# Three blocks of 512 tokens in place of four of 384 at the end of an attention-and-MLP kernel

## The chip, the cores and the metric

The kernel runs on one core of a Trainium2 chip. The metric is device time in microseconds (us), the median of several runs of the compiled program. Engines are named as in the profile: PE is TensorE (PEld its weight loads), DVE VectorE, ACT ScalarE, POOL GpSimd, SP SyncE, which issues nearly all DMAs here. Instructions of one engine start in the order in which they stand.

## What is computed

```python
# attention: 4 sequences of 768 tokens, 8 heads of 64; chunks of 32 queries, each with its own keys:
# 8 memory keys, 16 tokens to the left, the chunk itself, 8 tokens to the right (cut off at the ends)
scores = scale * np.matmul(q_c, k_full.transpose(0, 1, 3, 2))
a = np.exp(scores - np.max(scores, axis=-1, keepdims=True))
a = a / (np.sum(a, axis=-1, keepdims=True) + 1e-09)
out[:, :, c_start:c_end] = np.matmul(a, v_full)
# x: 3072 tokens x 512, then the MLP with 2048 hidden columns
h = x @ w_in
g = (a[0] + a[1]*h + a[2]*h**2 + a[3]*h**3) / (1 + abs(b[0])*abs(h) + abs(b[1])*h**2 + 1e-6)
return (g @ w_out).astype(np.float32)
```

All is float32 in and out. Weights and activations are split into a high and a low part, and each product of the MLP is three matmuls (high by high, low by high, high by low).

## The kernel before

**Blocks and steps.** The 3072 tokens are 8 blocks of 384, numbered 0 to 7. The hidden columns are 16 tiles of 128. One *step* n takes one block through one tile of hidden columns; there are 128 steps. Blocks 0 and 1 are done in two halves (10 and 6 tiles), so the order is: 0 and 1 (first ten tiles), 2, the rest of 1 (steps 36 to 41), the rest of 0 (42 to 47), then block 3 (48 to 63), 4 (64 to 79), 5, 6 and 7 (112 to 127).

**What one step does.** `g1(n)` is the in-projection: 12 matmuls (4 slices of 128 rows of x, 3 products each) that write the bank `h`, 128 hidden columns by the tokens of the block. The *chain* of step n makes g from h: ACT `chain_abs` (|h| and a line of it), POOL `chain_below` (the denominator, `cy`), ACT `chain_line` and DVE `chain_above` (the numerator, two instructions that read h), ACT `chain_inverse` (Ln and Exp, the reciprocal `cr`), DVE `chain_ratio` (three instructions that read the reciprocal), POOL `chain_hi` and `chain_lo` (`ghi`, `glo`, the split of g). `g2(n)` is the out-projection: for each 128 tokens three matmuls of 512 output columns into an accumulator `o`, with ghi, ghi and glo in that order. When a block's 16 tiles are through, `evac` copies the accumulators to a stage buffer and DMAs it out.

**The order, from step 30 on**, is written out in one loop, and all instructions are pinned to it:

```python
for n in range(HAND, LAST):
    g2(n - 2)
    attend(n, "db")          # attention on PE: values of one pair of heads, scores of another
    attend(n, "qv")          # loads
    g1(n + 1)
    ...
    chain_abs(n); chain_below(n); chain_line(n)     # evac of tiles `early` stands behind these
    chain_above(n); chain_inverse(n)                # evac of the other tiles behind these
    chain_ratio(n)
    chain_hi(n - 1); chain_lo(n - 1)
    attend(n, "xhlencmQ")
```

So PE runs g2(n-2), then g1(n+1), while the other engines work at the chain of n. The last six steps stand in `FINAL`, in the same manner.

**Attention between the steps.** From block 3 on the attention of a block is made while earlier blocks are in the MLP, one *unit* for each of its four pairs of heads. Its pieces, by the letters that `attend` takes: b scores (PE), m maximum and two subtractions (DVE), x exponential (ACT), c transpose on DVE and four DMAs that put the blocks in place, d values (PE), n normalisation (DVE: two small instructions for the reciprocal of the sum, two products), e transpose and DMAs, h and l the split of x (ACT, POOL). `BASES`, `LEAD`, `WHEN`, `AFTER` and `SOON` give each piece its step. A *visit* is a step in which PE has values or scores between g2 and g1; from step 40 on there are 18, of which the last two (101 and 105) have values alone. The values carry a column of ones, whose product is the sum over keys. Q, q and v load a unit's queries and keys into one half of the tile `qk_pairs` (by turns) and its values into one of four half tiles `v_main`.

**Banks.** Eight banks of 512 floats per partition: three for `o`, two for `h` (by turns), one for `cr`, two for `pairs` (scores and values).

Of the kernel before, what the change touches and what calls it, by code (L numbers as in the profile page):

```python
# [12 lines left out]
F32 = mybir.dt.float32  # L13
# [6 lines left out]
CHUNK = 32  # L20
# [12 lines left out]
BLOCKWISE = 3  # L33
BASES = {3: [30, 32, 35, 37], 4: [40, 42, 46, 50]}
# [25 lines left out]
LAST = 122  # L60
# [10 lines left out]

@with_exitstack
def attn_moe(ctx, tc, qk, vm, w, ab, out):
    nc = tc.nc
    P = 128
    NBLK, NPAIR = qk.shape[:2]
    NJT, DM = w.shape[0], out.shape[1]
    D = DM // (2 * NPAIR)
    TB = out.shape[0] // NBLK
    NC = TB // CHUNK  # L80
    NG = TB // P
    KEYS = P // 2
    NK, NQ, NV = start_of(NC - 1) + KEYS, NC * CHUNK, NC * (D + 1)
    NCT = DM // P
# [6 lines left out]
    st = ctx.enter_context(tc.tile_pool(name="st", bufs=3))  # L91
# [22 lines left out]
    v_mains = [const.tile([P, 2, NV], F32, name=f"v_main{i}") for i in range(2)]  # L114
# [187 lines left out]
    def pair_max(i, p):  # L302
        u = unit[i, p]
        sv = u.pop("s")
        mx = sm.tile([P, 2, NG], F32, name="mx")
        pin(nc.vector.tensor_reduce(mx, sv, axis=AX.X, op=ALU.max))
        e = u["e"] = at.tile([P, NG, KEYS, 2], F32, name="e", tag="e", bufs=2)
        turned = e.rearrange("x g w h -> x g (w h)").rearrange("x g (b h k) -> x g b h k", b=4, h=2)
        for h in range(2):
            pin(nc.vector.tensor_tensor(turned[:, :, :, h], sv[:, h].rearrange("x g (b k) -> x g b k", b=4),  # L310
                                        mx[:, h].unsqueeze(2).unsqueeze(3).broadcast_to([P, NG, 4, KEYS // 4]), op=ALU.subtract))

    def pair_values(i, p):
        u = unit[i, p]
        ov = u["o"] = two_banks("o", D + 1)
# [429 lines left out]
```

## Time and profile before

| | |
|---|---|
| device time, median of 3 runs | 618.96 us (618.54 to 621.61) |
| span of the profiled execution, first to last instruction | 617.3 us |
| busy share of the span | PE 98%, PEld 86%, DVE 79%, ACT 71%, POOL 70% |

The profile shows one execution; its own device time isn't listed beside its span, and the median of the runs lies 1.7 us above that span. An engine's busy time is the union of its instructions. Where the mean time of a matmul is shown, it is from start to end, and matmuls overlap: the time that PE needs for each is read from the starts.

### The profile page before, as it was taken

The numbers are of one execution on the slowest core, as the hardware profiler recorded it, in microseconds if no ns is written. First come the engines' busy times: TensorE is split into PE (matmuls) and PEld (weight loads), VectorE is DVE, ScalarE is ACT, GpSimd is POOL, SyncE is SP. The second block draws the span as 40 slices with busy tenths as digits, with TensorE's granted clock in tenths as the row PEclk, the third lists the DMA queues.
The fourth block names the chain that finished last, engine by engine and source line by source line (L and its number), as shares of the span: only waits on it lengthen the run. The fifth ranks groups of instructions, "written<-read, shape, count | busy, mean of one in ns | idle before, by whom it ended". The sixth has DMA issues, their size and how long they took to land.

```text
span 617.3 us, 14116 instructions
## 1 busy us (share of the span) xinstructions
PE 602.5 (98%) x5275; PEld 531.3 (86%) x5275; DVE 490.2 (79%) x959; ACT 435.6 (71%) x822; POOL 433.2 (70%) x459
## 2 busy tenths in 40 slices
PE   7699999999999999999999999999999999999997
PEld 5478789899888888889889898888989888989996
DVE  6799998898867889788778787777878777666674
ACT  5699888798756766666667766676676766676674
POOL 2569987879966667666767766766767676776773
PEclk9999999999999999999999999999999999999999
DMA  8979437103023564342221422242112310010001
GB/s 261 362 267 357 171 104 258 51 1 145 2 83 86 180 209 146 119 132 81 82 81 35 122 68 72 81 133 82 47 54 69 98 27 14 14 52 2 0 1 51
DMA packets 42787, 64.81 MB, mean 105 GB/s; under 512 B 25696, under 2 KB 25696, under 8 KB 42336
## 3 DMA queue, kind: packets, MB, share of 16 engines
q1 hardware_dynamic: 41856, 60.61, 30.7%
q10 hardware_dynamic: 576, 1.74, 0.9%
q0 software_dynamic: 288, 1.57, 0.8%
q8 instruction: 41, 0.67, 0.5%
q14 instruction: 26, 0.21, 0.1%
HBM read 46.60 MB, written 9.44 MB: 91 GB/s over the span
## 4 chain that ended last, share of the span: by engine, by line
PE 28%; issue 28%; POOL 27%; DVE 6%; DMA 5%; ACT 3%; SPq 1%; POOLq 0%; DVEq 0%
PE o L468 13%; PE h L453 13%; POOL glo L542 11%; POOL ghi L535 10%; POOL cy L509 3%; DMA w_raw<-in_w_dram 2%; POOL x_lo L431 2%; DMA out_dram<-stage 2%; POOL w_hl L189 1%; SPq L124 1%; DMA v_main<-in_vm_dram 1%; DVE ct L528 1%; PE pa L393 1%; DVE ct L518 1%; DVE ct L530 1%
## 5 line engine op out<-in xcount | busy, mean ns | idle before, releaser
L453 PE MATMUL h<-x_hi,w_hl 128*128 128x384 f32 x1024 | 265.4, 340 | 1.0 <-DVE ct L519 0.5
L468 PE MATMUL o<-w_hl,ghi 128*128 128x512 f32 x768 | 239.6, 393 | 0.0
L509 POOL TENSOR_TENSOR cy<-cy,ha 128x384 f32<-128x384 f32 x128 | 130.6, 1020 | 140.1 <-ACT cy L505 135.4
L453 PEld LDWEIGHTS h<-x_hi,w_hl 128*128 128x128 f32 x1024 | 185.6, 188 | 12.5 <-DVE ct L519 2.1
L453 PE MATMUL h<-x_lo,w_hl 128*128 128x384 f32 x512 | 172.6, 337 | 0.0
L468 PEld LDWEIGHTS o<-w_hl,ghi 128*128 128x128 f32 x768 | 141.8, 188 | 20.9 <-POOL glo L542 0.4
L468 PE MATMUL o<-w_hl,glo 128*128 128x512 f32 x384 | 151.3, 394 | 0.1
L542 POOL TENSOR_TENSOR glo<-ct,ghi 128x384 fp32r<-128x384 f32 x127 | 129.1, 1017 | 8.9
L504 ACT ACTIVATE ha<-h 128x384 f32<-128x384 f32 x128 | 62.9, 492 | 91.7 <-PE h L453 87.2
L518 DVE TENSOR_TENSOR ct<-ct,h 128x384 f32<-128x384 f32 x128 | 70.5, 551 | 58.4 <-ACT ct L514 58.2
L528 DVE SCALAR_TENSOR_TENSOR ct<-ct,par,cr 128x384 f32<-128x384 f32 x128 | 78.5, 613 | 38.5 <-ACT cr L524 37.5
L535 POOL TENSOR_TENSOR ghi<-ct,zero 128x384 fp32r<-128x384 f32 x127 | 105.6, 831 | 3.7 <-DVE ct L530 2.6
L523 ACT ACTIVATE cr<-cy 128x384 f32<-128x384 f32 x128 | 63.2, 494 | 58.9 <-POOL cy L509 54.5
L453 PEld LDWEIGHTS h<-x_lo,w_hl 128*128 128x128 f32 x512 | 96.2, 188 | 0.0
L505 ACT ACTIVATE cy<-ha,bab 128x384 f32<-128x384 f32 x128 | 91.0, 711 | 4.2
L468 PEld LDWEIGHTS o<-w_hl,glo 128*128 128x128 f32 x384 | 72.0, 187 | 21.1 <-POOL glo L542 1.9
L514 ACT ACTIVATE ct<-h,par 128x384 f32<-128x384 f32 x128 | 84.2, 658 | 0.1
L519 DVE SCALAR_TENSOR_TENSOR ct<-ct,par,h 128x384 f32<-128x384 f32 x128 | 78.7, 615 | 4.5
L530 DVE SCALAR_TENSOR_TENSOR ct<-cr,ct 128x384 f32<-128x384 f32 x128 | 71.4, 558 | 4.4
L529 DVE SCALAR_TENSOR_TENSOR cr<-cy,cr 128x384 f32<-128x384 f32 x128 | 71.0, 555 | 0.0
L524 ACT ACTIVATE cr<-cr 128x384 f32<-128x384 f32 x128 | 60.8, 475 | 4.0
L189 POOL TENSOR_TENSOR w_hl<-w_raw,w_hl 128x512 fp32r<-128x512 f32 x32 | 42.2, 1321 | 7.3 <-ACT w_hl L184 7.3
(65 smaller groups left out, 409.2 us busy)
## 6 DMA issues: line engine op xcount, KB each, us to landing
w_raw<-in_w_dram SPq DMA_DIRECT2D x26, 512.0 KB, 6.9
v_main<-in_vm_dram SPq DMA_DIRECT2D x20, 390.0 KB, 4.7
qk_pairs<-in_qk_dram SPq DMA_DIRECT2D x16, 424.0 KB, 4.0
out_dram<-stage SPq DMA_DIRECT2D x24, 256.0 KB, 3.2
qk<-in_qk_dram SPq DMA_DIRECT2D x24, 212.0 KB, 5.2
v_main<-in_vm_dram SPq DMA_DIRECT2D x20, 195.0 KB, 5.8
eT<-blocks SPq DMA_DIRECT2D x80, 48.0 KB, 2.0
xf<-blocks SPq DMA_DIRECT2D x80, 48.0 KB, 2.0
```

What stands on the lines that cost most here:

```text
L453: pin(nc.tensor.matmul(h[:, :TB], lhsT=wt[:, cols], rhs=xt[i][:, ct, :], start=m == 0, stop=m == last))
L468: ins = nc.tensor.matmul(o, lhsT=gt[:, cols], rhs=wt, start=begin and m == 0, stop=end and m == 2)
L505: pin(nc.scalar.activation(c["y"], c["ha"], AF.Identity, scale=B1, bias=B0))
L509: pin(nc.gpsimd.tensor_tensor(c["y"], c["y"], c.pop("ha"), op=ALU.mult))
L514: pin(nc.scalar.activation(c["t"], c["h"], AF.Identity, scale=A3, bias=A2))
L518: pin(nc.vector.tensor_tensor(t, t, h, op=ALU.mult))
L519: pin(nc.vector.scalar_tensor_tensor(t, t, A1, h, op0=ALU.add, op1=ALU.mult))
L528: pin(nc.vector.scalar_tensor_tensor(t, t, A0, r, op0=ALU.add, op1=ALU.mult))
L529: pin(nc.vector.scalar_tensor_tensor(r, yy, QC, r, op0=ALU.add, op1=ALU.mult))
L530: pin(nc.vector.scalar_tensor_tensor(t, r, 2.0, t, op0=ALU.subtract, op1=ALU.mult, reverse0=True))
L535: pin(nc.gpsimd.tensor_tensor(ghi, chain[z]["t"], zero.broadcast_to([P, TB]), op=ALU.add))
L542: pin(engine.tensor_tensor(glo, chain.pop(z)["t"], gh[z].bitcast(F32), op=ALU.subtract))
```

## The change

The last 1536 tokens become three blocks of 512 (`WIDE = 4`: blocks 4, 5 and 6); blocks 0 to 3 stay at 384. There are 112 steps; blocks 4, 5 and 6 have steps 64 to 79, 80 to 95 and 96 to 111. In a wide step the bank `h` is filled, and g2 has four accumulators; the fourth takes the bank that was `cr`. The reciprocal of a wide step is written over `h` itself, and from step 98 (`FREE`) into the `pairs` bank, which has no attention left. A wide unit has 16 chunks. With its values no column of ones is loaded, because the normalisation's reciprocal comes from a sum over the exponentials on DVE (`pair_sums`, letter z); keys that don't exist at the ends of a sequence are set to zero on POOL (`absent`). In wide steps some attention pieces stand at other places of the loop, and the pieces of three units of block 4 are given steps by hand (`ALONE`). To make room, the stage buffers are one tile and the free ends of `v_main` and `qk_pairs`; `v_main` are two rooms and not four; a wide unit's queries and keys take the whole of `qk_pairs`; the DMA scratch is 1 KB; and x of block 0, which is kept in DRAM for a while, is loaded back by ACT's queue and not POOL's (`x_move`).

```diff
+WIDE = 4
+BLOCKS = [384] * WIDE + [512] * 3
-WHEN = dict(b=0, m=1, x=2, c=2)
+WHEN = dict(b=0, m=1, x=2, c=2, z=3)
-SOON = {3: (dict(m=0, x=1, c=1), dict(e=1, h=4, l=4)), 4: (dict(m=0), {})}
+SOON = {3: (dict(m=0, x=1, c=1), dict(e=1, h=4, l=4)), 4: (dict(m=0, z=3), {})}
+ALONE = {(4, 0): dict(z=45), (4, 1): dict(m=44, x=45, c=45, z=47, h=56, l=56), (4, 2): dict(x=49, c=51, z=52)}
-LAST = 122
+LAST = 106
+FREE = 98
...
-                pin(nc.gpsimd.dma_start(out=t, in_=d))
+                pin(nc.scalar.dma_start(out=t.bitcast(F32), in_=d.bitcast(F32)))
...
+    def pair_sums(i, p):
+        if i < WIDE:
+            return
...
+        for h in range(2):
+            pin(nc.vector.tensor_reduce(sums[:, h], turned[:, h], axis=AX.XY, op=ALU.add))
+        u["rinv"] = inverse_of(sums.unsqueeze(3), n)
...
     def chain_inverse(y):
-        r = chain[y]["r"] = ps_r.tile([P, 512], F32, name="cr", tag="cr")[:, :TB]
+        i = order[y][0]
+        r = chain[y]["h"]
+        if i < WIDE:
+            r = ps_r.tile([P, 512], F32, name="cr", tag="cr")[:, :TB]
+        elif y >= FREE:
+            r = ps_pairs[0].tile([P, 2, 512], F32, name="pairs", tag="pairs")[:, 0]
+        chain[y]["r"] = r
         pin(nc.scalar.activation(r, chain[y]["y"], AF.Ln, bias=QC))
         pin(nc.scalar.activation(r, r, AF.Exp, scale=-1.0))
...
-        early = {True: [0, 1], False: [0]}[order[n - 2][0] < 2]
+        early = [0] if order[n - 2][0] in (2, 3) else [0, 1]
         chain_abs(n)
         chain_below(n)
         chain_line(n)
+        wide = order[n][0] >= WIDE
+        if wide:
+            attend(n, "xh")
         if done_block:
             evac(*done_block, early)
         chain_above(n)
+        if wide:
+            attend(n, "czm")
         chain_inverse(n)
...
-        attend(n, "xhlencmQ")
+        attend(n, "lenQ" if wide else "xhlenczmQ")
```

On PE, in the last steps, the end of one in-projection and the out-projection behind it were, before (h and o are the banks, x_hi and x_lo the split x, w_hl the split weights; a step has the pair of h rows four times):

```order
L453 MATMUL h<-x_hi_103,w_hl 128x384 x2
L453 MATMUL h<-x_lo_105,w_hl 128x384
L468 MATMUL o_7418<-w_hl,ghi 128x512 x2
L468 MATMUL o_7418<-w_hl,glo 128x512
L468 MATMUL o_7419<-w_hl,ghi 128x512 x2
L468 MATMUL o_7419<-w_hl,glo 128x512
L468 MATMUL o_7420<-w_hl,ghi 128x512 x2
L468 MATMUL o_7420<-w_hl,glo 128x512
```

On PE, at the same place of a wide step, they are now:

```order
L510 MATMUL h<-x_hi_102,w_hl 128x512 x2
L510 MATMUL h<-x_lo_104,w_hl 128x512
L526 MATMUL o_6729<-w_hl,ghi 128x512 x2
L526 MATMUL o_6729<-w_hl,glo 128x512
L526 MATMUL o_6730<-w_hl,ghi 128x512 x2
L526 MATMUL o_6730<-w_hl,glo 128x512
L526 MATMUL o_6731<-w_hl,ghi 128x512 x2
L526 MATMUL o_6731<-w_hl,glo 128x512
L526 MATMUL o_6732<-w_hl,ghi 128x512 x2
L526 MATMUL o_6732<-w_hl,glo 128x512
```

The 12 matmuls into h are 512 columns wide and not 384; the out-projection has four accumulators of three matmuls, and no shape of it changed.

On DVE, the step that holds a unit's maximum was, before (ct is the numerator and then g, cr the reciprocal, e the scores less their maximum, mx):

```order
L518 TENSOR_TENSOR ct<-ct,h 128x384
L519 SCALAR_TENSOR_TENSOR ct<-ct,par,h 128x384
L528 SCALAR_TENSOR_TENSOR ct<-ct,par,cr 128x384
L529 SCALAR_TENSOR_TENSOR cr<-cy,cr 128x384
L530 SCALAR_TENSOR_TENSOR ct<-cr,ct 128x384
L306 TENSOR_REDUCE mx<-pairs 128x6
L310 TENSOR_TENSOR e<-pairs,mx 128x12x16 x2
```

On DVE, the same step of a wide block is now:

```order
L591 TENSOR_TENSOR ct<-ct,h 128x512
L592 SCALAR_TENSOR_TENSOR ct<-ct,par,h 128x512
L333 TENSOR_REDUCE mx<-pairs 128x8
L337 TENSOR_TENSOR e<-pairs,mx 128x16x16 x2
L607 SCALAR_TENSOR_TENSOR ct<-ct,par,h 128x512
L608 SCALAR_TENSOR_TENSOR h<-cy,h 128x512
L609 SCALAR_TENSOR_TENSOR ct<-h,ct 128x512
```

The reciprocal is read from h, and the maximum moved from behind the ratio to between the numerator and the ratio.

On DVE, at the end of step 42 and in step 43, where block 1's accumulators are added to their kept halves (stage), there stood before (xt is the normalised result, blocks what a transpose writes):

```order
L331 TENSOR_TENSOR xt<-pairs,rinv 128x3x16x4 x2
L364 STREAM_TRANSPOSE blocks<-e 128x384
L306 TENSOR_REDUCE mx<-pairs 128x6
L310 TENSOR_TENSOR e<-pairs,mx 128x12x16 x2
L492 SCALAR_TENSOR_TENSOR stage<-o_2862,stage 128x512
L492 SCALAR_TENSOR_TENSOR stage<-o_2863,stage 128x512
L518 TENSOR_TENSOR ct<-ct,h 128x384
```

On DVE, at that place, there stand now:

```order
L374 TENSOR_TENSOR xt<-pairs,rinv 128x3x16x4 x2
L421 STREAM_TRANSPOSE blocks<-e 128x512
L559 SCALAR_TENSOR_TENSOR v_main_100<-o_2860,v_main_100 128x512
L559 SCALAR_TENSOR_TENSOR v_main_101<-o_2861,v_main_101 128x512
L591 TENSOR_TENSOR ct<-ct,h 128x384
```

The maximum of unit (4, 1) and its two subtractions left this place; they stand behind the ratio of step 44 now.

## Rows read from the trace of the kernel before

**Rows 1.** The page, busy time of each engine.
```profile
PE 602.5 (98%) x5275; PEld 531.3 (86%) x5275; DVE 490.2 (79%) x959; ACT 435.6 (71%) x822; POOL 433.2 (70%) x459
```

**Rows 2.** Timeline, PE, 521 to 613 us: start, duration, engine, line, operation.
```profile
521.32 0.51 PE L453 MATMUL h<-x_hi,w_hl 128*128 128x384 f32 x2
...
585.97 0.62 PE L468 MATMUL o<-w_hl,ghi 128*128 128x512 f32 x2
...
588.03 0.51 PE L453 MATMUL h<-x_hi,w_hl 128*128 128x384 f32 x2
...
603.07 0.63 PE L468 MATMUL o<-w_hl,ghi 128*128 128x512 f32 x2
...
613.08 0.39 PE L468 MATMUL o<-w_hl,glo 128*128 128x512 f32 x1
```

**Rows 3.** Timeline, PE, around a full visit and one with values alone.
```profile
406.27 0.62 PE L468 MATMUL o<-w_hl,ghi 128*128 128x512 f32 x2
...
411.75 0.63 PE L468 MATMUL o<-w_hl,ghi 128*128 128x512 f32 x2
...
514.24 0.62 PE L468 MATMUL o<-w_hl,ghi 128*128 128x512 f32 x2
...
516.39 0.73 PE L318 MATMUL pairs<-v_main,eT 64*32 64x65 f32 x48
517.04 0.62 PE L453 MATMUL h<-x_hi,w_hl 128*128 128x384 f32 x2
...
519.24 0.63 PE L468 MATMUL o<-w_hl,ghi 128*128 128x512 f32 x2
```

**Rows 4.** Timeline, ACT, POOL and DVE, one step behind its h; brackets: idle time, releaser.
```profile
586.16 0.49 ACT L504 ACTIVATE ha<-h 128x384 f32<-128x384 f32 x1 [0.80 <-PE h L453]
...
587.30 0.65 ACT L514 ACTIVATE ct<-h,par 128x384 f32<-128x384 f32 x1
...
587.48 1.02 POOL L509 TENSOR_TENSOR cy<-cy,ha 128x384 f32<-128x384 f32 x1 [1.27 <-ACT cy L505]
...
587.99 0.56 DVE L518 TENSOR_TENSOR ct<-ct,h 128x384 f32<-128x384 f32 x1 [0.91 <-ACT ct L514]
...
588.45 0.84 POOL L535 TENSOR_TENSOR ghi<-ct,zero 128x384 fp32r<-128x384 f32 x1
588.53 0.50 ACT L523 ACTIVATE cr<-cy 128x384 f32<-128x384 f32 x1 [0.58 <-POOL cy L509]
588.58 0.61 DVE L519 SCALAR_TENSOR_TENSOR ct<-ct,par,h 128x384 f32<-128x384 f32 x1
...
589.37 1.01 POOL L542 TENSOR_TENSOR glo<-ct,ghi 128x384 fp32r<-128x384 f32 x1
589.57 0.62 DVE L528 SCALAR_TENSOR_TENSOR ct<-ct,par,cr 128x384 f32<-128x384 f32 x1 [0.37 <-ACT cr L524]
...
590.69 0.56 DVE L530 SCALAR_TENSOR_TENSOR ct<-cr,ct 128x384 f32<-128x384 f32 x1
```

**Rows 5.** Groups by line: 512 columns on POOL, DVE, ACT (busy us, mean ns, idle before).
```profile
L189 POOL TENSOR_TENSOR w_hl<-w_raw,w_hl 128x512 fp32r<-128x512 f32 x32 | 42.2, 1321 | 7.3 <-ACT w_hl L184 7.3
...
L177 DVE SCALAR_TENSOR_TENSOR w_raw<-w_raw,stage 128x512 uint32<-128x512 uint32 x32 | 22.1, 690 | 1.1
...
L495 ACT ACTIVATE stage<-o 128x512 f32<-128x512 f32 x18 | 10.1, 594 | 2.3 <-PE o L468 2.1
```

**Rows 6.** Groups by line: a unit's maximum and subtractions on DVE.
```profile
L310 DVE TENSOR_TENSOR e<-pairs,mx 128x192 f32<-128x192 f32 x40 | 12.4, 353 | 0.7
...
L306 DVE TENSOR_REDUCE mx<-pairs 128x6 f32<-128x384 f32 x20 | 10.8, 542 | 0.0
```

**Rows 7.** Timeline, step 43: the ratio ends late, POOL and then PE wait.
```profile
241.90 0.83 POOL L535 TENSOR_TENSOR ghi<-ct,zero 128x384 fp32r<-128x384 f32 x1 [0.39 <-DVE ct L530]
...
243.18 0.63 PE L468 MATMUL o<-w_hl,ghi 128*128 128x512 f32 x2
...
245.62 0.51 PE L453 MATMUL h<-x_hi,w_hl 128*128 128x384 f32 x2
```

More of the change, by code (lines that the diff above doesn't have):

```diff
@@ L112, in attn_moe @@
     nc.gpsimd.memset(zero, 0.0)
-    v_mains = [const.tile([P, 2, NV], F32, name=f"v_main{i}") for i in range(2)]
+    v_rooms = [const.tile([P, 2 * NV], F32, name=f"v_main{i}") for i in range(2)]
+    v_mains = [t.rearrange("x (h n) -> x h n", h=2) for t in v_rooms]
     in_order = [True]
@@ L277, in places, with room @@
     def places(i):
-        return [(g, j, 4 * g + j if i < BLOCKWISE else NG * j + g) for g in range(NG) for j in range(4)]
+        n = sizes(i)[2]
+        return [(g, j, 4 * g + j if i < BLOCKWISE else n * j + g) for g in range(n) for j in range(4)]
+    def room(pool, name, dtype, tag, bufs):
+        return pool.tile([P, TW], dtype, name=name, tag=tag, bufs=bufs)
     def across(blocks, name):
-        t = at.tile([P, TB], F32, name=name, tag=name, bufs=XB.get(name, 1))
-        n = TB // 4
+        words = blocks.shape[1]
+        t = room(at, name, F32, name, XB.get(name, 1))[:, :words]
+        n = words // 4
         for j in range(4):
@@ L474, in fetch, with stage, evac @@
         for t in range(NG):
-            y = st.tile([P, DM], F32, name="stage", tag="stage")
+            y = stage(i)
             load(y, part[i][t * P:(t + 1) * P, :])
             kept.append(y)
-    def evac(i, j, tiles=range(NG)):
-        for t in tiles:
+    stages = [st.tile([P, DM], F32, name="stage", tag="stage")] + [t[:, NCW * D:NCW * D + DM] for t in v_rooms]
+    staged = [0]
+    def stage(i):
+        if i >= BLOCKWISE and len(stages) == NG:
+            stages.append(qk_bufs["pairs"][:, NKW + TW:NKW + TW + DM])
+        staged[0] += 1
+        return stages[staged[0] % len(stages)]
+    def evac(i, j, tiles=None):
+        for t in range(sizes(i)[2]) if tiles is None else tiles:
             rows = slice(t * P, (t + 1) * P)
@@ L493, in evac, with chain_of @@
             else:
[L494 removed]
+                y = stage(i)
                 pin(nc.scalar.mul(y, o, 1.0 / W_SCALE))
[L496 removed]
+            load(out[AT[i] + t * P:AT[i] + (t + 1) * P, :], y)
     spares = []
+    def chain_of(x):
+        if x not in chain:
+            chain[x] = {"h": hps.pop(x)[:, :BLOCKS[order[x][0]]]}
+        return chain[x]
     def chain_abs(x):
[L501 to L503 removed]
+        n = BLOCKS[order[x][0]]
+        c = chain_of(x)
+        c["y"] = room(tp, "cy", F32, "cy", 2)[:, :n]
+        c["ha"] = room(tp, "ha", F32, "ha", 1)[:, :n]
         pin(nc.scalar.activation(c["ha"], c["h"], AF.Abs))
@@ L532, in chain_hi @@
     def chain_hi(z):
-        ghi = gh[z] = gp.tile([P, TB], F32R, name="ghi", tag="ghi") if z < total - 4 else at.tile([P, TB], F32R, name="ghi", tag="xf", bufs=2)
+        n = BLOCKS[order[z][0]]
+        ghi = gh[z] = (room(gp, "ghi", F32R, "ghi", 2) if z < total - 4 else room(at, "ghi", F32R, "xf", 2))[:, :n]
         if z < total - 1:
-            pin(nc.gpsimd.tensor_tensor(ghi, chain[z]["t"], zero.broadcast_to([P, TB]), op=ALU.add))
+            pin(nc.gpsimd.tensor_tensor(ghi, chain[z]["t"], zero.broadcast_to([P, n]), op=ALU.add))
         else:
@@ L725, in lay_out, with lay_out_wide @@
     vm[BLOCKWISE:] = late.swapaxes(3, 4).reshape(vm[BLOCKWISE:].shape)
-    return qk, vm
+    return qk[:WIDE], vm[:WIDE], *lay_out_wide(q, kp, vp[..., :D], S)
+def lay_out_wide(q, kp, vp, S):
+    B, H, D = len(q), q.shape[1], q.shape[3]
+    span, keys = RUN * CHUNK, WIN + MEM
+    qk, vm = [], []
+    for i in range(WIDE, len(BLOCKS)):
+        kt, qt, vt = [], [], []
+        for at in range(sum(BLOCKS[:i]), sum(BLOCKS[:i + 1]), span):
+            b, first = at // S, at % S // CHUNK
+            rows = spread(first, RUN, S)
+            kt.append(kp[b][:, rows])
+            qt.append(q[b][:, first * CHUNK:first * CHUNK + span])
+            vt += [vp[b][:, rows[start_of(c):start_of(c) + keys]] for c in range(RUN)]
+        one = np.concatenate(kt + qt, axis=1)
+        qk.append(one.reshape(H // 2, 2, -1, D).transpose(0, 1, 3, 2))
+        n = len(vt)
+        rows_of = np.stack(vt, axis=2).reshape(H // 2, 2, 4, keys // 4, n * D)
+        vm.append(rows_of.swapaxes(2, 3).reshape(H // 2, 2, keys, n * D))
+    return np.stack(qk), np.stack(vm)
 def kernel(q, k, v, mem_k, mem_v, moe_w_in, moe_w_out, moe_a, moe_b):
```

151 lines of the change are left out of this document (92 added, 59 removed).

## The prediction, made before the changed kernel was run

> **What bounds the kernel now.** I read the page's busy times first [rows 1]: PE is busy 98% of the span, and no other engine is over 86%. A busy PE doesn't show that it is never late, since its matmuls overlap. So I then read the starts on PE's timeline, where a wait would show as a step that is longer than its neighbours. From the first matmul of one in-projection at 521.32 to that at 588.03 there are 16 steps [rows 2], none with a visit: 66.71 / 16 = 4.169 us each. In one of them the out-projection takes 588.03 - 585.97 = 2.06, so the in-projection takes 2.11. At the end five out-projections follow one another: 45 starts from 603.07 to 613.08, 10.01 / 44 = 0.2275 us for a matmul of 512 columns, with nothing between. Nine of these are 2.05, so a step's out-projection waits for nothing, and changing from h to o or back costs about 0.01. This stretch is PE from end to end, and what shortens PE's work shortens the kernel, as long as no other engine comes in late. How near they are to that is the second question, and [rows 4] answers it below.
>
> **1. The matmuls.** Out-projection: four blocks x 16 steps x 9 are 576 matmuls of 512 columns, three blocks x 16 x 12 are 576 of the same. No gain. In-projection: 64 x 12 = 768 of 384 columns become 48 x 12 = 576 of 512. A matmul of 384 takes 2.11 / 12 = 0.176, one of 512 0.2275 [rows 2]: 128 columns more cost 0.052, so 0.176 is 0.155 for the columns and some 0.02 for being a matmul. 192 matmuls fewer save that much each. In whole steps: before, 64 x 4.169 = 266.8. After, 24 x 0.2275 plus two changes of about 0.0125 are 5.485, x 48 = 263.3. **Gain 3.5.** Bounds: with 2.06 / 9 = 0.2289 for each of the 24 a step is 5.494 and the gain 3.1; with no cost of changing, 5.46 and 4.7.
>
> Here the trace and the Trainium skill differ. Its page TensorE: Matmul & The Clock Gate, in Back-to-back issue gap, gives the isolated gap as the columns at 2.4 GHz plus 2.5 ns. By that 384 columns take 162.5 ns and 512 take 215.8, an estimate from that page; the saving would be 16 x (48 x 162.5 - 36 x 215.8) ns = 0.5 us. The rows show 176 and 227.5, so I go by them.
>
> **2. The visits.** A unit of 12 chunks has 48 small matmuls for its scores and 48 for its values; four units become three of 64 and 64, so the number of small matmuls stays. The visits become fewer: 18 before from step 40 on; after, steps 40, 42, 46, 50 and 53 to 81 by fours, with 85 and 89 for values alone, 14. A full visit stretches the time from one out-projection to the next to 411.75 - 406.27 = 5.48, one with values alone to 519.24 - 514.24 = 5.00 [rows 3], 1.31 and 0.83 over a plain step. So 48 small matmuls cost 0.48 and the visit itself 0.35, if values and scores cost the same; if not, 48 values take 517.04 - 516.39 = 0.65 and the visit itself only 0.18. Four visits fewer: 1.4 or 0.7. **Gain 1.0.**
>
> **3. Step 43.** DVE has block 1's additions there, the ratio ends late, POOL waits 0.39 for it, and PE's out-projection takes 245.62 - 243.18 = 2.44, 0.38 too long [rows 7]. The change takes a maximum and two subtractions (542 and twice 353 ns [rows 6], partly overlapped) out of DVE's queue just ahead of these additions. They stand behind the ratio of step 44 now, and step 45 has a transpose and the new sums. Steps 44 and 45 have no visit to hide that, but ghi of a step isn't begun before POOL has the next `cy`, so a ratio may end over a microsecond late for nothing. **Gain 0.2**, bounds 0.4 (all of the wait) and -0.8 (it comes back at 44 and 45).
>
> **4. What the wide chain costs PE: nothing, if it is in time.** Two deadlines decide. Times are from the end of h, which is the start of the next out-projection (585.97 [rows 2]).
> *The bank h.* Before, h was free when the numerator had read it. Now it is free after the ratio, and the order excerpt shows the maximum between the two. The numerator ends at 589.19 - 585.97 = 3.22 [rows 4], Ln to ratio is 589.57 - 588.53 = 1.04, the ratio ends 591.25 - 589.57 = 1.68 later. Ln can no longer begin beside the numerator, since it writes what that reads, so the three add up. For 512 columns the rows give 690 ns for a DVE instruction that takes some 610 at 384, 594 for ACT against 490, 1321 for POOL against 1020 [rows 4, 5]. With +0.1 for each of six instructions ahead of the numerator's end and +0.1 for each of the five behind it, 3.8 + 1.2 + 2.0 = 7.0; with everything at 4/3, 7.9. The bank is needed by the in-projection after next: one step and one out-projection, 5.485 + 2.74 = 8.2. In the step with the maximum, 0.54 + 0.71 at 4/3 is 1.66 in place of Ln and Exp's 1.2 to 1.4: 7.5 to 8.2. In time, by 0.7 or by nothing.
> *glo.* POOL's glo ends at 590.38 - 585.97 = 4.41 [rows 4] and is wanted by the third matmul of the next out-projection, 4.169 + 0.455 = 4.62: 0.2 to spare. At 512 POOL starts at 1.51 + 0.2, and three instructions with 0.3 more each end at 5.5; with all at 4/3, 5.9. Wanted at 5.94. In time too. The sums on DVE fall between numerator and ratio, where DVE waits for ACT anyway. The zeroing memsets on POOL stand ahead of ghi in five wide steps; below they cost nothing, above (at ghi's 0.84 each step) they would make glo late by some 0.4, five times: 2.
> I take 0. Step by step, an engine that is late for one step has its idle time in the next to come back (DVE idles 0.91 and 0.37 in the step shown [rows 4]).
>
> **5. The rest at nothing.** The single buffer for queries and keys: a load begins behind a unit's scores and the next scores are two steps (over 8 us) or four on. The x load on ACT's queue: two issues in one step's idle time (0.80 and more [rows 4]), and their lanes' earlier DMAs are steps old. The fourth tile's evacuation: ACT takes 0.594 for one [rows 5], PE 0.68 for a tile's three matmuls, at the end too, so the tail behind the last matmul stays. The DMA scratch serves nothing that remains.
>
> **Sum:** -3.5 - 1.0 - 0.2 = -4.7. The profiled span of 617.3 would be 612.6; 1.7 lies around it to the median. **614.3 us.**
>
> **Rivals.**
> *A. Only the columns count.* If a matmul of 512 columns costs 4/3 of one of 384, 0.176 x 4/3 = 0.234, the in-projection gains nothing, and terms 2 and 3 leave 617.8. Against it: both sizes are measured in the same stretch, though the 512 one with w and not x as its moving operand. By the gap rule of the Trainium skill's page TensorE: Matmul & The Clock Gate, above, it would be 617.3.
> *B. DVE is late in narrow steps that carry wide units* (44 to 63). A unit's share of DVE grows by a third and by the sums, in steps that are no longer than before. For it: step 43 [rows 7] shows how such lateness reaches PE. Three to eight waits of 0.4 cost 1.2 to 3: 615.5 to 617.5.
> *C. Slower: the bank h is late in wide steps.* If the ratio ends s after the deadline, each of 46 steps waits s, since the next one starts from there. It eats the gain at s = 0.1 and makes the kernel slower by over 0.5% at s = 0.17, with the ratio at 8.4. For it: everything at 4/3 comes to 7.9 to 8.2. Against it: no instruction of [rows 5] is at 4/3. With s = 0.2: 614.3 + 9 = 623.5.
> *D. The memsets make glo late:* 616.3.
>
> **Chances.** A measurement of this kernel can tell about 0.5% from no change: 615.9 and 622.1 are the marks. Forecast 0.66 (its own range 613.0 to 615.6 from the bounds of terms 1 to 3), A 0.06, B 0.16, C 0.08, D 0.04. Of B a quarter lies below 615.9, of C half is above 622.1 and half between. Faster 0.70, same 0.25, slower 0.05. The range holds the forecast, A, B and D: 612.9 to 617.9.
>
> **What would show it.** Right: plain wide steps of 5.47 to 5.50 on PE's timeline; 576 in-projection matmuls with starts 0.228 apart; 14 visits; no wait of PE for DVE's third ratio instruction in the list of waits; step 43's out-projection near 2.1. Wrong: wide steps with a pause ahead of h (C) or inside o after two matmuls (glo, D), or pauses in steps 44 to 56 (B). The forecast fails as a whole if the 512-column in-projection, whose moving operand is x and not w, doesn't run at the out-projection's 0.2275.

## The result, and the profile after

| | before | after | after, built and run a second time |
|---|---|---|---|
| device time, median | 618.75 us (618.48 to 621.61) | 611.63 us (610.93 to 613.53) | 609.90 us (609.76 to 610.28) |
| ratio to before, 95% interval | | 0.9885 [0.9859, 0.9911] | 0.9854 [0.9829, 0.9879] |
| span of the profiled execution | 617.3 us | 609.9 us | 608.5 us |

The kernel is 7.1 us faster, where 4.7 were forecast: the side is right, and the size lies 1.3 us outside the range. A second measurement of the same kernel, beside its own runs of before, had a median 1.7 us lower. Its profiled span is 1.4 lower: 0.9 of that is a stop of PE, which experiments 8 and 9 are about, and 0.5 lies ahead of step 40.

The page after: the busy times (before: [rows 1]), the chain that ended last by engine, and two of the costliest groups (busy us, mean ns, idle time ahead and its releaser).

```profile
PE 592.8 (97%) x5083; PEld 502.4 (82%) x5083; DVE 486.5 (80%) x867; ACT 416.6 (68%) x734; POOL 424.0 (70%) x421
...
PE 89%; DMA 6%; POOL 2%; SPq 1%; issue 1%; ACT 1%; DVE 1%; POOLq 0%
...
L602 ACT ACTIVATE h<-cy 128x512 f32<-128x512 f32 x34 | 20.5, 602 | 45.1 <-DVE ct L592 43.6
...
L607 DVE SCALAR_TENSOR_TENSOR ct<-ct,par,h 128x512 f32<-128x512 f32 x34 | 25.2, 740 | 27.8 <-ACT h L603 27.8
```

PE has 9.7 us less to do and is still the bound. ACT's Ln now waits for the numerator, 43.6 us in all, as it must where the reciprocal is written over h; PE doesn't feel it.

To find where the time went I cut both traces at the first in-projection of steps 40 and 64. Busy time of each engine in the two stretches (window, length, busy times), first of before, then of after.

```profile
217.45:327.64 110.19, 110.11 (x1178) 97.73 (x1177) 91.14 (x188) 71.36 (x134) 75.67 (x81) 1.00 0.39 116
327.64:617.30 289.66, 285.69 (x2323) 255.52 (x2321) 215.08 (x420) 193.06 (x360) 194.45 (x207) 1.00 0.19 54
```

```profile
216.75:330.16 113.41, 112.44 (x1369) 99.85 (x1368) 100.33 (x201) 72.53 (x134) 77.20 (x89) 1.00 0.43 130
330.16:609.86 279.70, 276.03 (x1939) 226.62 (x1937) 201.86 (x315) 172.97 (x272) 185.05 (x163) 1.00 0.16 46
```

Ahead of step 40 the kernel after is 0.7 earlier. From 40 to 64, where narrow steps carry the wider units, it loses 3.2; from 64 on it gains 10.0. In the second run of the same kernel these are -1.2, +2.3 and -10.0: only the first two move from run to run. The clock granted to TensorE is 1.00 in all stretches, the higher of its two levels (2.4 GHz).

**Plain steps.** PE's timeline after (start, duration, engine, line, operation): the in-projections of steps 91 and 107, sixteen steps apart, and around a full visit (answers to [rows 2, 3]).

```profile
362.58 0.61 PE L526 MATMUL o<-w_hl,ghi 128*128 128x512 f32 x2
363.03 0.39 PE L526 MATMUL o<-w_hl,glo 128*128 128x512 f32 x1
363.35 0.80 PE L345 MATMUL pairs<-v_main,eT 64*32 64x64 f32 x60
...
364.76 0.73 PE L510 MATMUL h<-x_hi,w_hl 128*128 128x512 f32 x2
...
486.29 0.39 PE L510 MATMUL h<-x_hi,w_hl 128*128 128x512 f32 x1
...
573.38 0.39 PE L510 MATMUL h<-x_hi,w_hl 128*128 128x512 f32 x1
```

87.09 / 16 = 5.443 us for a step, 0.2268 for each of 24 matmuls, h and o alike; most steps are 5.440. I had 5.485.

**The wide chain.** One step of it on all engines, in the order of time (answers to [rows 4]).

```profile
494.45 0.62 PE L526 MATMUL o<-w_hl,ghi 128*128 128x512 f32 x2
...
496.80 0.69 DVE L591 TENSOR_TENSOR ct<-ct,h 128x512 f32<-128x512 f32 x1
...
497.52 0.75 DVE L592 SCALAR_TENSOR_TENSOR ct<-ct,par,h 128x512 f32<-128x512 f32 x1
...
498.36 0.60 ACT L602 ACTIVATE h<-cy 128x512 f32<-128x512 f32 x1 [1.60 <-DVE ct L592]
...
499.61 0.75 DVE L607 SCALAR_TENSOR_TENSOR ct<-ct,par,h 128x512 f32<-128x512 f32 x1 [1.34 <-ACT h L603]
...
501.00 0.69 DVE L609 SCALAR_TENSOR_TENSOR ct<-h,ct 128x512 f32<-128x512 f32 x1
...
502.61 0.62 PE L510 MATMUL h<-x_hi,w_hl 128*128 128x512 f32 x2
...
503.99 1.29 POOL L622 TENSOR_TENSOR glo<-ct,ghi 128x512 fp32r<-128x512 f32 x1
...
505.33 0.62 PE L526 MATMUL o<-w_hl,ghi 128*128 128x512 f32 x2
```

h ends where the out-projection starts, 494.45. The numerator ends 3.82 later (worked out: 3.8), the ratio 501.69 - 494.45 = 7.24 later (7.0 to 7.9), and the in-projection that needs the bank starts at 8.16 (8.2): 0.9 to spare. glo ends at 505.28, and the third matmul of the out-projection of 505.33 wants it at 505.79: 0.5 to spare, or 0.3 for its weight load, which begins at 505.56. Over all steps from 64 to 97 the ratio ends 7.23 to 7.61 behind h, also where the maximum stands ahead of it, and at least 0.9 ahead of the in-projection.

glo isn't in time everywhere. In step 68 two of the memsets that set absent keys to zero stand on POOL ahead of ghi, and a weight load of PE waits for glo.

```profile
352.75 0.12 POOL L408 MEMSET e<- 32x32 f32 x1
352.95 1.04 POOL L615 TENSOR_TENSOR ghi<-ct,zero 128x512 fp32r<-128x512 f32 x1
...
355.40 0.19 PEld L526 LDWEIGHTS o<-w_hl,glo 128*128 128x128 f32 x1 [0.25 <-POOL glo L622]
```

This step takes 5.574, 0.13 over a plain one. Steps 72, 80 and 84, with one memset each, take 5.47, and step 76 takes 5.440 with one too.

**A stop that nobody forecast.** PE's timeline in step 51 after: the only gap over 0.4 us between starts on PE from step 40 on.

```profile
269.16 0.62 PE L510 MATMUL h<-x_hi,w_hl 128*128 128x384 f32 x2
270.75 0.45 PE L510 MATMUL h<-x_lo,w_hl 128*128 128x384 f32 x1 [0.96 <-issue]
```

Two matmuls into h run, and the third starts 1.30 behind the second; the step takes 5.51 where its like takes 4.27, so 1.2 is lost. The releaser reads "issue": no semaphore, engine or DMA of the program is waited for.

### The profile page after: what moved, and what is told of

It is laid out like the page before. It is cut to its first block, busy times and chain, and to the rows that moved or that the text cites. A ratio compares the mean times of both kernels' runs of the same rounds, so it can differ in the third digit from the quotient of the medians.

```text
span 609.9 us, 13371 instructions
## 1 busy us (share of the span) xinstructions
PE 592.8 (97%) x5083; PEld 502.4 (82%) x5083; DVE 486.5 (80%) x867; ACT 416.6 (68%) x734; POOL 424.0 (70%) x421
## 3 DMA queue, kind: packets, MB, share of 16 engines
q10 hardware_dynamic: 1632, 3.47, 1.7%
## 4 chain that ended last, share of the span: by engine, by line
PE 89%; DMA 6%; POOL 2%; SPq 1%; issue 1%; ACT 1%; DVE 1%; POOLq 0%
PE h L510 42%; PE o L526 41%; DMA qk<-in_qk_dram 4%; DMA w_raw<-in_w_dram 2%; PE pairs L345 2%; PE pairs L325 2%; SPq L141 1%; PE pa L385 1%; PE pa L450 1%; POOL w_hl L206 1%; POOL glo L622 0%; POOL cy L582 0%; PE pa L473 0%; POOL ghi L615 0%; PE pa L432 0%
## 5 line engine op out<-in xcount | busy, mean ns | idle before, releaser
L510 PE MATMUL h<-x_hi,w_hl 128*128 128x384 f32 (+1 forms) x896 | 252.1, 362 | 0.9 <-DVE ct L592 0.8
L582 POOL TENSOR_TENSOR cy<-cy,ha 128x384 f32<-128x384 f32 (+1 forms) x112 | 127.4, 1138 | 140.8 <-ACT cy L578 137.4
L510 PE MATMUL h<-x_lo,w_hl 128*128 128x384 f32 (+1 forms) x448 | 161.1, 360 | 1.0 <-issue 1.0
L622 POOL TENSOR_TENSOR glo<-ct,ghi 128x384 fp32r<-128x384 f32 (+1 forms) x111 | 125.6, 1132 | 7.6
L577 ACT ACTIVATE ha<-h 128x384 f32<-128x384 f32 (+1 forms) x112 | 60.2, 537 | 82.3 <-PE h L510 79.7
L615 POOL TENSOR_TENSOR ghi<-ct,zero 128x384 fp32r<-128x384 f32 (+1 forms) x111 | 101.9, 918 | 4.4 <-DVE ct L609 2.2
L591 DVE TENSOR_TENSOR ct<-ct,h 128x384 f32<-128x384 f32 (+1 forms) x112 | 67.8, 605 | 45.9 <-ACT ct L587 45.7
L578 ACT ACTIVATE cy<-ha,bab 128x384 f32<-128x384 f32 (+1 forms) x112 | 84.6, 756 | 3.7
L587 ACT ACTIVATE ct<-h,par 128x384 f32<-128x384 f32 (+1 forms) x112 | 78.7, 702 | 0.1
L592 DVE SCALAR_TENSOR_TENSOR ct<-ct,par,h 128x384 f32<-128x384 f32 (+1 forms) x112 | 75.2, 672 | 4.0
L602 ACT ACTIVATE h<-cy 128x512 f32<-128x512 f32 x34 | 20.5, 602 | 45.1 <-DVE ct L592 43.6
```

The lines of the kernel that those rows point to most:

```text
L510: pin(nc.tensor.matmul(h[:, :BLOCKS[i]], lhsT=wt[:, cols], rhs=xt[i][:, ct, :], start=m == 0, stop=m == last))
L577: pin(nc.scalar.activation(c["ha"], c["h"], AF.Abs))
L578: pin(nc.scalar.activation(c["y"], c["ha"], AF.Identity, scale=B1, bias=B0))
L582: pin(nc.gpsimd.tensor_tensor(c["y"], c["y"], c.pop("ha"), op=ALU.mult))
L587: pin(nc.scalar.activation(c["t"], c["h"], AF.Identity, scale=A3, bias=A2))
L591: pin(nc.vector.tensor_tensor(t, t, h, op=ALU.mult))
```

## The experiments

The diffs are shortened. The runs of experiments 1 to 6 and 11 to 14 are single ones and are read from their traces.

**1 and 2: is it POOL, or the weight load?** In plain steps before, the starts inside h are 0.171 to 0.185 apart for the first six matmuls and 0.173 behind them, those inside o 0.234 at first and 0.227 at the end. The regular pace, 12 x 0.1733 + 9 x 0.2267, would be a step of 4.120 and not 4.169. Two theories of the 0.05: a glo that is only just in time (POOL), or a weight load of 188 ns that doesn't fit under 173 (LOAD). The loads, in plain steps before and with experiment 2 (busy us, mean ns, idle ahead):

```profile
L453 PEld LDWEIGHTS h<-x_hi,w_hl 128*128 128x128 f32 x129 | 23.7, 188 | 1.3
```

```profile
L454 PEld LDWEIGHTS h<-x_hi,w_hl 128*64 128x64 f32 x57 | 7.6, 134 | 0.5
```

```diff
 def chain_below(x):          # experiment 1, on the kernel before
+    if x >= 64: return
```

> The kernel before, with POOL's product for the denominator (cy times ha) left out from step 64 on, so that its output has another denominator there. POOL is 1.0 us earlier in each of these steps and glo, which was 0.2 us ahead of its use, is over 1 us ahead. Theory POOL (the 0.05 us by which a plain step before, 4.169, is longer than 12 x 0.1733 + 9 x 0.2267 = 4.120 comes from weight loads that stand behind a glo that is only just in time): plain steps of 4.12, and about 3 us less in all. Theory LOAD (a weight load of 188 ns is longer than the 173 ns between two matmuls of 384 columns, so PE has no room to catch up): plain steps stay at 4.16 to 4.17 and the time within 0.7 us of the kernel before.

```diff
-    nc.tensor.matmul(h[:, :TB], lhsT=wt[:, cols], ...        # experiment 2, on the kernel before
+    k = 64 if n >= 64 and m % 3 and m < last else P
+    nc.tensor.matmul(h[:k, :TB], lhsT=wt[:, ct * P:ct * P + k], ...
```

> The kernel before, with 64 in place of 128 weight columns in seven of the twelve in-projection matmuls from step 64 on (they leave out half of their output rows); the 384 moving columns stay. Theory LOAD: if a load of 64 columns is shorter than 173 ns, the starts inside h become regular at 0.1733, those of o at 0.2267, and a plain step is 4.12. Theory POOL: the chain keeps its times, so a plain step stays at 4.17.

Measured: with POOL light 66.98 / 16 = 4.186 a step (steps 107 to 123), 618.41 us; with short loads 66.53 / 16 = 4.158, 617.79 us. POOL is out: the step didn't fall, and a glo that is early left the starts inside o between 0.224 and 0.236. The short loads took 134 ns, and h came near its pace (0.1735 on average), but o stayed irregular (mostly 0.224 to 0.241, 0.2307 on average). LOAD explains a fifth of the 0.05 at most.

**3 and 4: 384 or 448 columns back in a wide step.**

```diff
-    nc.tensor.matmul(h[:, :BLOCKS[i]], lhsT=wt[:, cols], rhs=xt[i][:, ct, :], ...
+    nc.tensor.matmul(h[:, :MOVED], lhsT=wt[:, cols], rhs=xt[i][:, ct, :MOVED], ...   # wide blocks; the chain has 384
```

> The kernel after, but the in-projection of the wide blocks moves only 384 of the 512 columns, the chain works on 384, and the fourth 128 tokens of the out-projection use the first 128 again (128 columns of each wide step are left out). The loads stay, glo has about 0.8 us to spare. Theory LOAD: the matmuls into h start 0.1755 apart and irregularly, the first of o 0.229 to 0.234, a plain wide step is 12 x 0.1755 + 12 x 0.228 = 4.84 or more. Theory POOL: 12 x 0.1733 + 12 x 0.2267 = 4.80, regular.

> As the run with 384 moved columns, but with 448: a matmul of 448 columns is expected at 0.1867 + 0.0133 = 0.200, longer than the load of 188 ns. Theories LOAD and POOL both expect 12 x 0.200 + 12 x 0.2267 = 5.12 with regular starts; LOAD expects the irregularity of 384 columns to be gone here. If starts are irregular here too, neither the load nor a late glo makes them so.

PE's timeline of the run with 384: the in-projections of steps 91 and 97.

```profile
470.49 0.33 PE L511 MATMUL h<-x_hi,w_hl 128*128 128x384 f32 x1
...
499.69 0.33 PE L511 MATMUL h<-x_hi,w_hl 128*128 128x384 f32 x1
```

29.20 / 6 = 4.867: the irregular starts are back (h 0.171 to 0.185, the first nine of o 0.224 to 0.236, the last three 0.227), in a kernel where glo ends 0.7 us ahead of the load that takes it (472.15 and 472.83). So the extra belongs to PE's matmuls and not to what feeds them. With 448 a step is 5.166 and not 5.12, with starts of 0.199 to 0.207 in h: LOAD, which expected these to be regular, is wrong here.

**5 and 6: one width in a step.** MIX (a change of width costs) against ROOM (a load needs more room than 448 columns leave).

```diff
-    nc.tensor.matmul(o, lhsT=gt[:, cols], rhs=wt, ...
+    nc.tensor.matmul(o[:, :MOVED], lhsT=gt[:, cols], rhs=wt[:, :MOVED], ...
```

> As the run with 448 moved columns, but in wide steps the out-projection moves 448 of its 512 columns too (64 output columns are left out, except in a block's first and last step), so that all 24 matmuls have one width. Theory MIX (starts are irregular only where matmuls of one width follow those of another): regular starts 0.200 apart, plain steps of 24 x 0.200 = 4.80. Theory ROOM (a load of 188 ns needs more room under a matmul than 448 columns leave it, whatever stands ahead): starts as in the run with 448, 0.2025 on average or more, plain steps of 4.86 or more.

> As before with 384 columns in both products of wide steps (128 output columns left out). Theory MIX: regular starts 0.1733 apart, plain steps of 24 x 0.1733 = 4.16. Theory ROOM: the lag that a mixed step pays back in its 512-column matmuls has no such place here, so starts are 0.1755 or more, steps of 4.21 or more, up to 24 x 0.188 = 4.51 if the load sets the pace alone. glo is wanted at 4.5 and ends at 4.4, so a wait of PE for glo of up to 0.2 may stand beside either.

Measured: with 448 steps of 4.860 or 4.960 and starts of 0.1985 to 0.207, as ROOM said. With 384 the shortest steps are 4.160 and 4.167, fifteen lie under 4.21, and away from waits the starts are 0.173 to 0.174, as MIX said. The longer steps hold waits of PE's loads for glo, twelve of them, up to 0.6 where up to 0.2 was expected; behind one the starts are irregular again for some six matmuls. Each theory holds for one width and fails for the other.

**11: four changes of width in a step.**

```diff
-    g2(n - 2); attend(n, "db"); attend(n, "qv"); g1(n + 1)
+    g2(n - 2, first half); g1(n + 1, first half); g2(n - 2, second half)      # from step 98
+    attend(n, "db"); attend(n, "qv"); g1(n + 1, second half)
```

> As the run with 384 moved columns, but from step 98 on PE takes half of the out-projection, half of the in-projection, the other half of each: four changes of width in a step and not two; the matmuls are the same. Steps 90 to 97 of the same trace are the control. Theory MIX (the time over 12 x 0.1733 + 12 x 0.2267 = 4.800 comes from changing between widths, 0.066 a step with two changes): about 4.93 with four. Rival COUNT (each matmul of 384 columns costs its extra, wherever it stands): 4.87 as in the control. A pause ahead of the in-projection would be the bank h, asked for 1.4 us earlier, and is left out of the reading.

PE's timeline: the in-projections of steps 92 and 97 (two changes a step), and of 99 and 105 (four).

```profile
474.69 0.33 PE L513 MATMUL h<-x_hi,w_hl 128*128 128x384 f32 x1
...
499.03 0.33 PE L513 MATMUL h<-x_hi,w_hl 128*128 128x384 f32 x1
...
507.39 0.33 PE L513 MATMUL h<-x_hi,w_hl 128*128 128x384 f32 x1
...
536.61 0.33 PE L513 MATMUL h<-x_hi,w_hl 128*128 128x384 f32 x1
```

24.34 / 5 = 4.868 and 29.22 / 6 = 4.870: the same. Two more changes of width add nothing to a step, and MIX, which had 0.066 for each two, falls. COUNT has the sum right, but not where it stands. Of the 0.067 over 4.800, with two changes 0.027 lie in the starts of the 384s and 0.040 in those of the 512s; with four, 0.007 and 0.059. And where one in-projection follows another, so that no 512s stand ahead of its 384s, these start 0.1733 apart and the step is 0.026 shorter. Experiment 3 has such a place in step 109 (from its in-projection to that of step 110):

```profile
555.33 0.33 PE L511 MATMUL h<-x_hi,w_hl 128*128 128x384 f32 x1
...
560.17 0.33 PE L511 MATMUL h<-x_hi,w_hl 128*128 128x384 f32 x1
```

That is 4.84 and not 4.867. So the extra comes with both widths by turns, and not with 384 columns wherever they stand. The irregular starts of the 512s (0.233, 0.236, 0.224, 0.231, 0.236, 0.228) aren't peculiar to two widths: the kernel after has the same sequence behind its visits, among matmuls of 512 columns alone (step 70).

**13 and 14: other widths.** Three widths in the three wide blocks, alone and beside 512.

> As the run with 448 columns in both products, but blocks 4, 5 and 6 move 416, 480 and 496 columns. LINEAR (columns at 2.4 GHz plus 13.3 ns, as 384 and 512 give) would be 0.1867, 0.2133 and 0.2200 from start to start, plain steps of 4.48, 5.12 and 5.28. Theory ROOM (the load of 188 ns needs some 20 to 40 ns more under a matmul): 416 is over LINEAR by the most, 480 by less, 496 hardly. Theory ALIGN (only whole multiples of 128 columns are regular, as 384 and 512 are and 448 is not): all three are over LINEAR by 2.5 to 7 ns, as 448 was, in no order of their width.

> As the run with 384 moved columns, but the in-projection of blocks 4, 5 and 6 moves 416, 480 and 496 columns and the out-projection 512. LINEAR would be plain steps of 4.96, 5.28 and 5.36. With 384 a step was 0.066 over it, with 448 it was 0.047. Theory ROOM: the excess falls from 416 to 496, and is under 0.01 at 496. Theory ALIGN: each is over by 0.03 or more, 496 too. In either case the extra of a mixed step is a property of the widths, since the chain has 384 columns and room throughout.

The run with one width: in-projections of steps 91 and 95 (480 columns), and of 99 and 105 (496).

```profile
471.02 0.38 PE L511 MATMUL h<-x_hi,w_hl 128*128 128x480 f32 x1
...
491.82 0.38 PE L511 MATMUL h<-x_hi,w_hl 128*128 128x480 f32 x1
...
513.08 0.38 PE L511 MATMUL h<-x_hi,w_hl 128*128 128x496 f32 x1
...
544.76 0.38 PE L511 MATMUL h<-x_hi,w_hl 128*128 128x496 f32 x1
```

20.80 / 4 = 5.200 for 480 and 31.68 / 6 = 5.280 for 496. The run beside 512: in-projections of steps 75 and 76 (416), and of 99 and 105 (496).

```profile
389.61 0.35 PE L511 MATMUL h<-x_hi,w_hl 128*128 128x416 f32 x1
...
394.57 0.35 PE L511 MATMUL h<-x_hi,w_hl 128*128 128x416 f32 x1
...
520.91 0.38 PE L511 MATMUL h<-x_hi,w_hl 128*128 128x496 f32 x1
...
553.07 0.38 PE L511 MATMUL h<-x_hi,w_hl 128*128 128x496 f32 x1
```

That is 4.96 for 416 and 32.16 / 6 = 5.360 for 496. All widths together, as the mean from start to start in plain steps, and what a step with 12 of them and 12 of 512 has over LINEAR (columns at 2.4 GHz plus 13.3 ns):

| moved columns | LINEAR, ns | alone, ns | step beside 512, over LINEAR |
|---|---|---|---|
| 384 | 173.3 | 173.3 to 175 | 0.066 |
| 416 | 186.7 | 186.7 to 188.3 | 0.000 |
| 448 | 200.0 | 202.5 to 206.7 | 0.046 |
| 480 | 213.3 | 216.7 | 0.040 |
| 496 | 220.0 | 220.0 | 0.000 |
| 512 | 226.7 | 226.7 | 0.000 |

Alone, 416 is at 188.3 in nearly all steps and at 186.7 in one. ROOM falls (416 leaves less room than 480, and has less extra in either run) and so does ALIGN (496 has none in either run, and 416 none beside 512). What makes 384 costly beside 512, and 448 and 480 costly anyhow, stays open.

**7: the edits taken at nothing.** On the kernel before: `dynamic_dma_scratch_size=1024`, and `nc.scalar` for `nc.gpsimd` in `x_move`.

> The kernel before with two of the edits that were taken at nothing: the DMA scratch of 1 KB and the load of block 0's x on ACT's queue and not POOL's. Theory NOTHING (the 0.7 us by which the kernel after stands ahead at step 10 is chance in the startup's loads): ratio 1.000, within 0.5 us of before, and step 10's in-projection at 81.2 as before. Theory SCRATCH: step 10's in-projection near 80.5, and 0.7 us less in all.

Measured: 618.33 against 618.86 us, ratio 0.9993 [0.9984, 1.0002]. Step 10's in-projection stands at 80.16, but in the profiles of all the runs it lies between 80.0 and 82.3 for kernels of either kind, so the 0.7 ahead of step 10 is chance, and these edits are worth nothing that can be measured.

**8 and 9: the stop in step 51.**

```diff
-    for _ in range(WARM):            # experiment 9; experiment 8 is the kernel after, unchanged
+    for _ in range(WARM + 10):
```

> The kernel after, unchanged, as the mark for the two runs beside it: 611.6 us, a stop of PE of 1.3 us in the in-projection behind the visit of step 50.

> The kernel after with 24 in place of 14 warm-up transposes at PE's start, which moves every later matmul 20 instructions (10 loads, 10 matmuls) further along in PE's instruction stream. Theory FETCH (the 1.3 us stop behind the visit of step 50 is PE waiting for a 16 KB piece of its instructions, whose transfer began 2 instructions ahead of a visit of 256): the transfer begins 22 instructions, some 2 us, ahead of that visit, the stop is gone or under 0.3, and the time is 1.0 to 1.3 us less than the kernel after. Theory STORES (three stores of 256 KB and the load of queries and keys at that moment hold PE up): the stop stays at 1.3 and so does the time.

First the kernel after in its first run: transfers of the queue that carries PE's instructions and of the one that carries most other DMAs, in 267 to 270 us (packets, MB, share of 16 engines' time). Then the second run, the same queues in 266.5 to 269.5, and PE's timeline. Then ten more warm-ups.

```profile
q1 hardware_dynamic: 413, 0.56, 55.1%
q8 instruction: 1, 0.02, 3.8%
```

```profile
q1 hardware_dynamic: 543, 0.82, 77.9%
q8 instruction: 1, 0.02, 2.0%
...
268.66 0.62 PE L510 MATMUL h<-x_hi,w_hl 128*128 128x384 f32 x2
269.33 0.45 PE L510 MATMUL h<-x_lo,w_hl 128*128 128x384 f32 x1
```

```profile
268.68 0.62 PE L510 MATMUL h<-x_hi,w_hl 128*128 128x384 f32 x2
269.14 0.33 PE L510 MATMUL h<-x_lo,w_hl 128*128 128x384 f32 x1
```

That the queue carries PE's instructions is inferred: it has 40 pieces of 16 KB on the page, one for every 250 or so of PE's records on average. In both runs a piece is begun 2 records ahead of the visit of step 50 (267.57 and 267.02 by the transfers' own records), and the visit's 128 matmuls with their loads are 256 records in 1.4 us. Of 3 x 16 = 48 us of the 16 engines, the piece took 0.038 x 48 = 1.8 us the first time and 0.020 x 48 = 1.0 the second, so it ended at 269.37 and 267.99. The third matmul of h starts 270.75 - 269.37 = 1.38 behind the piece's end in the one and 269.33 - 267.99 = 1.34 in the other, and again 1.34 in experiment 10 (end 269.75, start 271.09). The traces of experiments 3 to 6, 11, 13 and 14, whose kernels are the same up to here, have the stop too: a piece of 1.24 to 1.76 us begun at the same record, 0.46 to 1.32 between the two matmuls, and the third 1.04 to 1.41 behind the piece's end. With ten warm-ups more the piece is begun 22 records ahead, at 264.80, and the third matmul follows at 269.14 with no stop. FETCH holds, and STORES falls as a cause of its own: in the second run stores and loads keep the DMA engines no less busy around the piece, and the stop is short. What makes the piece take 1.0 or 1.8 us no run here shows. The stop cost 1.2 in the first run and 0.3 in the second. So experiment 8, expected at 611.6 us with a stop of 1.3, was no mark for a gain in time: experiment 9 took 609.68 us, ratio 0.9855 [0.9829, 0.988], and against the 609.90 of experiment 8 that is no difference that can be told. What ten more warm-ups show is the trace without a stop.

**10: the maximum back in step 42** (`m=44` taken out of `ALONE`).

> The kernel after with the maximum and two subtractions of unit (4, 1) back in step 42, ahead of block 1's additions, the rest as it is. Theory TERM 3 (their leaving made step 43's out-projection short): the out-projection that follows waits for glo again, 0.4 us or, as a wide unit's three are longer, up to 0.7. Rival: DVE's queue has room there now, and nothing changes. Either way the total moves by 0.1% at most, so the trace decides.

POOL and PE's weight loads of that run (answers to [rows 7]).

```profile
241.76 0.83 POOL L615 TENSOR_TENSOR ghi<-ct,zero 128x384 fp32r<-128x384 f32 x1 [0.57 <-DVE ct L609]
...
243.74 0.19 PEld L526 LDWEIGHTS o<-w_hl,glo 128*128 128x128 f32 x1 [0.56 <-POOL glo L622]
```

POOL waits 0.57 for the ratio and PE's load 0.56 for glo. The step of this wait is 4.58 and the one ahead 4.33, against 4.19 and 4.17 in the kernel after: 0.55 comes back. Term 3's mechanism is shown. The total, 611.81 us, has the stop of 1.27 in it too.

**12: what disturbs the visits before.**

```diff
-    att_load(i, p, nc.sync if kind == "q" else nc.scalar)      # on the kernel before
+    att_load(i, p, nc.scalar)
```

> The kernel before with all loads of queries and keys issued by ACT's queue and not SP's, so that each is issued ahead of the visit and not during its scores. Eight of the 14 full visits before take 1.08 to 1.11 us from the first small matmul to the last and the others 0.98, the extra standing in the scores 0.7 us after the visit's start, 0.15 to 0.2 behind SP's issue of such a load. Theory ISSUE (the load, or its issue, disturbs the scores): from step 50 on the visits take 0.98. Rival: they stay at 1.08 to 1.11 in about half of the cases.

Measured: 11 of 14 full visits take 1.10 to 1.12 and three 0.98, more than before and not fewer; 618.79 us. ISSUE falls. The transfers' records have another sign: all uneven visits from step 40 on (nine before, six after) have a burst of packets of 384 or 512 bytes under their scores, which is the size in which the blocks are put in place, and the six even full visits after have next to none. Before, five of the seven even ones have such a burst as well, and no run here moves the bursts; so the cause stays open.

## Why the side was right and the size was not

Against the first profile of after, whose span is 7.4 shorter where 4.7 were forecast:

| | forecast | measured |
|---|---|---|
| 1, plain steps | 3.5 | 64 x 4.169 - 48 x 5.443 = 5.5 |
| 2, visits | 1.0 | 1.7 |
| 3, step 43 | 0.2 | 0.4 |
| 4, the wide chain | 0 | -0.2 |
| 5, the rest | 0 | 0.7 at the start, by chance, and 0.5 at the end |
| step 51 | not seen | -1.2 |

These make 7.4. The 0.5 at the end are a wait of a weight load for the numerator in before's last in-projection, 0.3, which has no counterpart after, and 0.2 behind the last matmul. Without the chance at the start and without the stop the gain would be 7.9, 3.2 more than forecast, and 2.0 of these are term 1. The prediction's own range was too narrow as well: the bounds of terms 1 to 3, all taken on one side, are 612.5 to 616.0, and the result lies below these too.

**The step that failed is the size of term 1.** I took "24 x 0.2275 plus two changes of about 0.0125". The 0.2275 is the mean of before's last 45 matmuls, and the first ten of these, behind the last in-projection of 384, start 0.224 to 0.236 apart; the others stand at 0.2267. The 0.0125 is what a change between h and o seemed to cost before, where it is also a change of width; the new step holds one width, and its 24 starts are even across h and o. 24 x 0.0008 and 0.025 are 0.044 a step, 2.1 us over 48. The 192 matmuls fewer save 192 x 0.0133 = 2.6 of the 5.5; the other 2.9 are the extra of steps with 384 beside 512, which experiment 3 brings back in a kernel whose chain has room. Why the two widths by turns cost it stays open. My own bound with no cost of changing, a gain of 4.7, was the better reading.

The gap rule of the Trainium skill's page TensorE: Matmul & The Clock Gate (Back-to-back issue gap) gave 0.5 for this term. The trace differs: 173.3 ns for 384 columns and 226.7 for 512 are 13.3 over the columns' time and not 2.5. That part is paid per matmul, and the rule would have priced it too low.

**Term 2** had the right mechanism. A visit's edges, from the records' starts, are 0.318 from the last o to the first small matmul and 0.146 from the last small to h, 0.237 over a plain change; four visits fewer are 0.95. The steps behind visits, 0.10 to 0.17 over plain ones, give another 0.2, since they are fewer. The other 0.5 was not in the term: the 1632 small matmuls from step 40 on take 17.7 us in all before and 17.2 after. Before, 96 take 0.98 us, but 1.08 to 1.11 in eight of the 14 full visits from step 46 on; after, 128 take 1.27 in all five full visits of wide steps, but of five visits with 128 in narrow steps four are uneven (1.36 to 1.55). Experiment 12 tried one cause, in vain.

**Term 3**: the wait is gone, and step 45 is 4.19 where the same step before was 4.55; the maximum's new place costs nothing. **Term 4** had the bank h right: ratio 7.23 to 7.61, at least 0.9 to spare. It had glo right but for a few steps: two weight loads wait for it from step 64 on, 0.25 in step 68 and 0.2 in step 99. Of the rivals, A is excluded by the steps and C by the ratio's times. D came on a small scale: the steps with memsets lose 0.2 in all (0.13 in step 68, 0.03 in 72, 80 and 84) and not 2. B, DVE late in steps 44 to 63, didn't come: the 3.2 lost there are 32 more small matmuls in each of five visits (1.65), 16 in two (0.3), their unevenness (0.4) and the stop (1.2), less term 3.

**The stop** is a cost that the prediction has no term for. It came where a piece of PE's instructions is asked for just ahead of a visit with as many instructions as a piece holds. Before, two visits had a piece begun 3 and 7 records ahead, but their 192 records don't use one up, and nothing stopped. The Trainium skill's page Runtime: NRT & Kernel Launch (Instruction fetch mechanics) has PE's instructions arrive in blocks of 16 KiB, 256 instructions, with a cost that is mostly hidden. The size agrees with the trace; the cost here was 0.3 and 1.2 us in the two runs, at one place.

## What to carry to other kernels

Take the pace of an instruction from a stretch that looks as the new kernel will (one width, no neighbours of another shape), and look at the single starts ahead of the mean: a tail of 45 matmuls held ten that were still disturbed. Fewer, wider matmuls save a fixed part each, here 13 ns, and a width can have a pace of its own: try the exact width, since 448 columns alone cost up to 207 ns and 496 cost 220. Where a burst of small matmuls has some 250 instructions, look at where the instruction pieces fall; ten matmuls more at the start, with their loads, moved them here.

## What the runs showed of the hardware

- Float32 matmuls with a weight load each start, with one width in a step, at the columns' time at 2.4 GHz plus 13.3 ns for 384, 496 and 512 columns, and later for 416 (by 1.6 ns in nearly all steps), 448 (2.5 to 6.7 ns) and 480 (3.3 ns).
- 384 beside 512 costs 0.066 us in a step of 12 and 12, the same in halves by turns; 384s that follow 384s have none of it themselves. 416 and 496 beside 512 cost nothing.
- A weight load takes 188 ns for 128 columns and 134 for 64, and such loads run back to back, overlapped, under matmuls that start 173 apart.
- PE went on 1.04 to 1.41 us behind the end of the 16 KB piece that it stood waiting for, in ten traces.
